# V of a recurrent attention layer: four 32-column tiles of the array at once instead of full-width matmuls with half-empty rows

## The chip, the cores and the metric

The kernel runs on one core of a Trainium2 chip. The metric is the device time of one execution in microseconds, taken as the median of several runs. The kernel before has 3807.35 us (three runs, 3803.83 to 3814.33).

The engines are named as the profile names them: PE is TensorE (matmuls; PEld are its weight loads), DVE is VectorE, ACT is ScalarE, POOL is GpSimd, and SP is the engine whose queue issues the loads of the weights.

## The reference, cut to what matters

Four blocks follow one another on a sequence of 2048 tokens of width 640: A, B, A, B, each with a residual and a layer norm ahead of it. Both A blocks have the same weights, and so have both B blocks.

```python
# A: attention over segments of 32 tokens, with 8 recurrent memory rows (H = 32 heads of Dh = 192)
for s in range(n_seg):                                   # 64 segments
    h = concat([mem, x[s * 32:(s + 1) * 32]])            # 40 rows
    q, k, v = h @ Wq, h @ Wk, h @ Wv                     # each 640 -> 32 x 192
    p = softmax(mask(q @ k.T * scale))                   # 40 x 40 for each head
    o = (p @ v) @ Wo                                     # 32 x 192 -> 640
    mem = o[:8]; out[s] = o[8:]
# B: sliding attention (8 keys, every second one back), 32 heads of 20
q, k, v = split(x @ wqkv); x + attention(q, k, v) @ wo
```

The memory makes the segments of A a chain: segment s + 1 can't begin before segment s has its first 8 output rows. The weights of A (Wq, Wk, Wv, Wo, each 640 x 6144) don't fit on the chip beside the rest, so most of them are loaded again for every segment.

## The kernel before, in words

**Steps and lanes.** One step (`run`, L515 to L554) does segment s of the first A block (lane 0) and segment s - 2 of the second A block (lane 1) together, so that each weight that is loaded serves both lanes: 80 columns, 2 x 40 rows. There are 66 steps, and one more that only ends B. B of both lanes runs within the same step.

**Halves.** The weights of A are cut into 64 "halves" of 480 KB (128 x 1920 bf16): 32 for q and k, 16 for v, 16 for o. 26 of them stay on chip (RESIDENT, L81, spread evenly over the order of use); 38 are loaded in every step through a ring of seven buffers (`half`, L217 to L231). In the first step they come from the inputs and are written to a DRAM copy in the layout of the tiles (`Wr`, L228); afterwards they come from there (L230, on SP's queue). A load can start when the matmuls that read the old contents of its buffer are done.

**The order of a step** is written out by hand in `stages()` (L51 to L63), and TensorE's program follows it exactly. The other engines' instructions are put in order by a scheduler, which keeps to their dependencies. The pieces:

- `q` (16 times, L295): two halves, one of k and one of q, each 15 matmuls of 80 columns (L303); ScalarE evicts the result (L305).
- `s` (4 times, L307): the scores of four units for both lanes (L315, L321), in two other tile forms of the array. VectorE adds the mask (L325), takes the maximum (L327) and subtracts it (L328); ScalarE does the exp (L329); VectorE sums, inverts and scales into Pm (L331 to L333).
- `t` (4 times, L336): TensorE transposes Pm (L340); VectorE copies the upper 64 partitions, those of lane 0, into PT (L342), ScalarE the lower 64, those of lane 1 (L343). The other half of each column of PT stays zero.
- `v` (16 times, L345): one half of Wv. The stationary operand is the 128 columns of ST: two lanes of 64 slots each, of which 40 hold rows and 24 are empty. The moving operand is the weight, 384 columns wide, five matmuls over the contraction (L351). ScalarE evicts the even ones (L355), VectorE the odd ones (L357).
- `pv` (4 times, L360): P times V for four of the v results, in 64-column tiles (L368); ScalarE evicts to ot (L371).
- `o` (16 times, L374): the output projection, one half each (L385), summed in one PSUM tile, acc, over the whole step.
- `e`, `qkv`, `logits`, `wo`, `ln1`, `ln2`: the parts of B. The logits at L444 are computed in four 32-column tiles of the array, each with its own moving operand. Each of the five `e` makes a matmul (L470), a product and a sum on VectorE (L473, L475). GpSimd and VectorE each make one of the two products at L435.

At the end of a step VectorE writes acc's memory rows into the next step's ST (L395). `ln2` (`beta_x`, L495) writes lane 1's new rows there: it takes x2 from `wo` (L486), squares it on GpSimd (L273), sums on VectorE (L275), and needs a matmul, ScalarE's ln and exp and VectorE again (L278 to L292).

**Buffers that the prediction speaks of.** psA, three PSUM buffers, serves q, v and acc (acc holds one from the first `o` to the end of the step). psB, two, serves the parts of B and `t`. vp, six, holds the evicted v.

Of the kernel before, what the change touches and what calls it, by code (L numbers as in the profile page):

```python
# [10 lines left out]
BF16 = mybir.dt.bfloat16  # L11
F32 = mybir.dt.float32
ACT = mybir.ActivationFunctionType
ALU = mybir.AluOpType
# [5 lines left out]
P = 128  # L20
D = 640
NCH = 5
# [3 lines left out]
NM = 8  # L26
SEG = 32
LT = NM + SEG
SLOT = 64
NP_ = 16  # L30
UW = 384
HALF = NCH * UW
NQK = 5
# [12 lines left out]
N_HALVES = 64  # L46
N_RESIDENT = 26
# [2 lines left out]

def stages():  # L51

    plan = [("q", 0), ("q", 1), ("alpha", 0), ("q", 2), ("q", 3), ("ln1", 0)]
    plan += [("q", 4), ("s", 0), ("v", 0), ("q", 5), ("v", 1), ("qkv", 0), ("q", 6), ("t", 0), ("v", 2), ("q", 7), ("v", 3)]
    for g in (2, 3):
        i, j = 4 * g, 2 * (g - 2)
        extra = [[], [], [("logits", 0)], [("input", 0)], []] if g == 2 else [[("e", c)] for c in range(5)]
        plan += [("q", i), ("s", g - 1), ("pv", g - 2)] + extra[0] + [("v", i - 4)] + extra[1] + [("q", i + 1)] + extra[2]
        plan += [("o", 2 * j), ("o", 2 * j + 1)] + extra[3] + [("v", i - 3), ("q", i + 2), ("t", g - 1), ("v", i - 2)] + extra[4]
        plan += [("o", 2 * j + 2), ("o", 2 * j + 3), ("q", i + 3), ("v", i - 1)]  # L60
    plan += [("s", 3), ("pv", 2), ("v", 12), ("v", 13), ("wo", 0), ("o", 8), ("o", 9), ("v", 14), ("v", 15), ("t", 3)]
    plan += [("o", 10), ("ln2", 0), ("pv", 3), ("o", 11), ("store", 0)]
    return plan + [("o", k) for k in range(12, 16)]  # L63


PLAN = stages()


def consumption_order():

    order = []
    for what, i in PLAN:
        if what == "q":
            order += [2 * i, 2 * i + 1]
        elif what in "vo":
            order.append((32 if what == "v" else 48) + i)
    return order


ORDER = consumption_order()  # L80
RESIDENT = {ORDER[(2 * i + 1) * N_HALVES // (2 * N_RESIDENT)] for i in range(N_RESIDENT)}  # L81


def window(ap, l):
# [23 lines left out]
class Kernel:  # L108
    def __init__(self, ctx, tc, A_x, A_mem0, A_Wq, A_Wk, A_Wv, A_Wo, B_wqkv, B_wo, out):
        self.tc, self.nc = tc, tc.nc  # L110
        self.x = A_x[0, :, :]
        self.out = out[0, :, :]
        self.S = A_x.shape[1]
        self.n_seg = self.S // SEG
        self.Wq, self.Wk, self.Wv = (w.rearrange("d h e -> d (h e)") for w in (A_Wq, A_Wk, A_Wv))
        self.Wo = A_Wo.rearrange("h e d -> (h e) d")
        self.B_wqkv, self.B_wo, self.mem0 = B_wqkv, B_wo, A_mem0[0, :, :]
        pool = lambda name, bufs, **k: ctx.enter_context(tc.tile_pool(name=name, bufs=bufs, **k))
        self.cp = pool("consts", 1)
        self.res = pool("res", 1)  # L120
        self.ring = pool("ring", RING)
        self.dram = pool("dram", 1, space=DRAM)
        self.w1 = pool("w1", 1)
        self.w2 = pool("w2", 2)
        self.w3 = pool("w3", 3)
        self.vp = pool("vp", 6)
        self.psA = pool("psA", 3, space=PSUM)
        self.psS = pool("psS", 3, space=PSUM)
        self.psB = pool("psB", 2, space=PSUM)


    def constants(self):
# [12 lines left out]
        for u in range(2):  # L145
            r = slice(SLOT * u, SLOT * (u + 1))
            nc.gpsimd.affine_select(out=m1[r, :], in_=m1[r, :], compare_op=ALU.is_ge, fill=NEG, base=0,
                                    pattern=[[-1, LT]], channel_multiplier=1)
            nc.gpsimd.memset(m1[SLOT * u:SLOT * u + NM, :], 0.0)
        self.maskA = cp.tile([P, LT], BF16, name="maskA")  # L150
        nc.vector.tensor_copy(out=self.maskA[:, :], in_=m1[:, :])

# [23 lines left out]
        self.wqkv = cp.tile([P, NCH, 3 * D], BF16, name="wqkv")  # L176
        self.wo = cp.tile([P, NCH, D], BF16, name="wo")

        self.ST = [cp.tile([P, NCH, 2, SLOT], BF16, name=f"ST{i}") for i in range(2)]
        for t in self.ST:  # L180
            nc.gpsimd.memset(t[:], 0.0)
        self.QK = [cp.tile([P, 12 * LT + SLOT - LT], BF16, name=f"QK{i}") for i in range(NQK)]
        for t in self.QK:
            nc.gpsimd.memset(t[:, 12 * LT:], 0.0)
        self.Pm = [cp.tile([P, 4, 2, SLOT], BF16, name=f"Pm{i}") for i in range(2)]
        for t in self.Pm:
            nc.gpsimd.memset(t[:], 0.0)
        self.PT = [cp.tile([P, 4, 2, 2, LT], BF16, name=f"PT{i}") for i in range(2)]
        for t in self.PT:
            nc.gpsimd.memset(t[:], 0.0)  # L190
        self.zero = cp.tile([P, NCH, SEG], BF16, name="zero")
        nc.gpsimd.memset(self.zero[:], 0.0)
        self.m0T = cp.tile([P, NCH, NM], BF16, name="m0T")
# [101 lines left out]
    def qk(self, i):  # L295
        nc = self.nc
        st = self.ST[self.step % 2]
        ps = self.psA.tile([P, 6, 2, LT], F32, name="qk_ps", tag="A")
        for k in range(2):
            w = self.half(2 * i + k)[:, :].rearrange("p (c n) -> p c n", c=NCH)  # L300
            for m in range(3):
                for c in range(NCH):
                    nc.tensor.matmul(ps[:, 3 * k + m, :, :], lhsT=w[:, c, m * P:(m + 1) * P], rhs=st[:, c, :, 0:LT],  # L303
                                     start=(c == 0), stop=(c == NCH - 1))
        nc.scalar.copy(out=self.QK[i % NQK][:, 0:12 * LT], in_=ps[:, :, :, :].rearrange("p m l t -> p (m l t)"))  # L305

    def scores(self, g):  # L307
        nc = self.nc
# [8 lines left out]
        for j in range(4):  # L317
            q = self.QK[(4 * g + j) % NQK]
            for l in range(2):
                for h in range(2):  # L320
# [9 lines left out]
        sm = self.w2.tile([P, 8], F32, name="sm")  # L330
        nc.vector.tensor_reduce(out=sm[:, :], in_=sb[:, :, :], op=ALU.add, axis=AX.X)  # L331
        nc.vector.reciprocal(out=sm[:, :], in_=sm[:, :])
        nc.vector.tensor_tensor(out=self.Pm[g % 2][:, :, :, 0:LT].rearrange("p a l t -> p (a l) t"), in0=sb[:, :, :],  # L333
                                in1=sm[:, :].unsqueeze(2).to_broadcast([P, 8, LT]), op=ALU.mult)

    def p_transpose(self, g):  # L336
        nc = self.nc
        ps = self.psB.tile([P, 4, 2, SLOT], BF16, name="pt_ps", tag="B")
        for j in range(4):
            nc.tensor.transpose(out=ps[:, j, :, :].rearrange("p h q -> p (h q)"),  # L340
                                in_=self.Pm[g % 2][:, j, :, :].rearrange("p l t -> p (l t)"), identity=self.ident[:, :])
        nc.vector.tensor_copy(out=self.PT[g % 2][0:64, :, :, 0, :], in_=ps[0:64, :, :, 0:LT])  # L342
        nc.scalar.copy(out=self.PT[g % 2][64:128, :, :, 1, :], in_=ps[64:128, :, :, 0:LT])  # L343

    def v(self, i):  # L345
        nc = self.nc
        w = self.half(32 + i)[:, :].rearrange("p (c n) -> p c n", c=NCH)
        st = self.ST[self.step % 2]
        ps = self.psA.tile([P, UW], F32, name="v_ps", tag="A")
        for c in range(NCH):  # L350
            nc.tensor.matmul(ps[:, :], lhsT=st[:, c, :, :].rearrange("p l t -> p (l t)"), rhs=w[:, c, :],  # L351
                             start=(c == 0), stop=(c == NCH - 1))
        vt = self.vp.tile([P, UW], BF16, name="vt")
        if i % 2 == 0:
            nc.scalar.copy(out=vt[:, :], in_=ps[:, :])  # L355
        else:
            nc.vector.tensor_copy(out=vt[:, :], in_=ps[:, :])  # L357
        self.vts[i] = vt

    def pv(self, g):  # L360
        nc = self.nc
        for k in (2 * g, 2 * g + 1):
            ps = self.psS.tile([P, 2, 3, 2, LT], F32, name="o_ps", tag="S")
            for jj in range(2):
                i = 2 * k + jj
                vt = self.vts.pop(i)
                for (n, slot, h, col) in ((0, 0, 0, 0), (0, 1, 0, 64), (1, 0, 0, 128), (1, 1, 1, 192), (2, 0, 1, 256), (2, 1, 1, 320)):
                    nc.tensor.matmul(ps[64 * slot:64 * (slot + 1), jj, n, :, :], lhsT=vt[:, col:col + 64], rhs=self.PT[g % 2][:, i % 4, h, :, :],  # L368
                                     start=True, stop=True, tile_position=(0, 64 * slot))
            ot = self.w3.tile([P, 6, 2, LT], BF16, name="ot")  # L370
            nc.scalar.copy(out=ot[:, :, :, :], in_=ps[:, :, :, :, :].rearrange("p j n l t -> p (j n) l t"))  # L371
            self.ots[k] = ot
# [142 lines left out]
    def run(self):  # L515
# [6 lines left out]
        with tc.manual_schedule(engines={PE}):  # L522
# [7 lines left out]
            for s in range(n_steps + 1):  # L530
# [10 lines left out]
                for what, i in PLAN:  # L541
                    if what in attend and a:
                        attend[what](i)
                    elif what in local and b:
                        local[what]()
                    elif what == "e" and b:
                        self.b_expand(i)
                    elif what == "alpha" and a and s + 1 < self.n_seg:
                        self.alpha_x(s + 1)
                    elif what == "input" and s % 4 == 2 and 4 * (s // 4 + 1) < self.n_seg:  # L550
                        self.input_tile(s // 4 + 1)
# [57 lines left out]
```

## Time and profile before

| what | value |
|---|---|
| median of the runs | 3807.35 us |
| the profiled execution's own time | 3796.64 us |
| its span, from the first to the last instruction | 3794.9 us |
| instructions | 172,681 |
| granted TensorE clock, mean | 0.981 |
| from HBM | 1251.42 MB, 335 GB/s over the span |
| loads `wt<-Wr` of 480 KB, from issue to landing | 2470, median 5.8 us |
| end of a step (L395), first and last of 65 | 149.5 us and 3766.0 us |

The page of the profile gives, in its first part, the busy time of each engine with its share of the span and its number of instructions. Its third part has a line for each DMA queue: packets, megabytes, and the time of its packets as a share of 16 engines' span. Its fourth part follows the chain that ended last backwards from the last instruction, and gives the shares by engine; "issue" there is time in which the engine waited for nothing that the profile shows. A line of a group has its source line, engine, operation, what it writes and reads with shapes, its count, then busy time in us and mean ns of one, then the idle time of the engine just before its instructions, with what ended most of it. A line of the waits reads: who waited, for whom, us in total, times, longest. A line in order of time reads: start in us, length in us, engine, line, operation, count, and in brackets the idle time before it. A line of the chain in order of time reads: start, length, engine, what, line, count.

The mean of one matmul holds its latency, since matmuls are pipelined; the rate is read from the starts of successive ones.

### The profile page before, as it was taken

What the parts mean: (1) busy time and instruction counts of PE and PEld (TensorE: products, weight loads), DVE (VectorE), ACT (ScalarE), POOL (GpSimd) and SP (SyncE); (2) the same over time, 40 slices, a digit from 0 to 9 for tenths busy, and PEclk for the clock granted to TensorE, in tenths of its full rate; (3) what the DMA queues carried; (4) which work ended last, traced back from release to release, by engine and by line L of the source; (5) the groups of instructions that cost most, each with busy time, mean ns of one, the idle gap of its engine ahead of it and who ended that gap; (6) DMA issues with size and microseconds to landing.
All of it is one profiled execution on the core that took longest, in us unless ns stands there. A gap on an engine that the chain in (4) does not pass through costs nothing.

```text
span 3794.9 us, 172681 instructions
## 1 busy us (share of the span) xinstructions
PE 3450.5 (91%) x79035; PEld 2983.5 (79%) x79035; DVE 2024.0 (53%) x4660; ACT 1496.2 (39%) x3213; POOL 372.2 (10%) x475
## 2 busy tenths in 40 slices
PE   5799999999999999999999999999999999999997
PEld 3578887887878888788778887888888888788886
DVE  1255555545545555554555555555555555545555
ACT  1233443444434344343444344444444444444443
POOL 3110010010001001001000100100110010011000
PEclk7899999999999999999999999999999999999998
DMA  9999999999999999999999999999999999999995
GB/s 353 376 329 335 348 341 343 334 338 342 334 335 341 338 349 341 327 350 327 343 336 335 344 338 342 342 339 347 333 348 343 349 338 341 343 332 351 340 352 216
DMA packets 403275, 1283.93 MB, mean 338 GB/s; under 512 B 41704, under 2 KB 83312, under 8 KB 402544
## 3 DMA queue, kind: packets, MB, share of 16 engines
q1 hardware_dynamic: 397200, 1251.58, 91.8%
q0 software_dynamic: 3040, 18.68, 1.2%
q8 instruction: 617, 10.11, 1.1%
q10 hardware_dynamic: 2304, 2.62, 0.2%
q14 instruction: 114, 0.93, 0.1%
HBM read 1251.42 MB, written 21.30 MB: 335 GB/s over the span
## 4 chain that ended last, share of the span: by engine, by line
PE 74%; DVE 16%; DMA 5%; issue 4%; ACT 1%; SPq 1%; POOLq 0%; POOL 0%; ACTq 0%
PE qk_ps L303 26%; PE v_ps L351 20%; PE acc L385 12%; DVE oT L475 5%; DVE prodv L473 4%; PE qkv_ps L428 4%; PE o_ps L368 3%; PE s_ps L321 3%; PE s_ps L315 3%; DMA x_sb<-in_A_x_dram 2%; DVE vt L357 2%; PE y_ps L482 1%; DMA wt<-in_A_Wq_dram 1%; ACT PT L343 1%; DVE sb L325 1%
## 5 line engine op out<-in xcount | busy, mean ns | idle before, releaser
L305 ACT CAST QK<-qk_ps 128x480 bf16<-128x480 f32 x1056 | 588.3, 557 | 1254.0 <-PE qk_ps L303 1243.2
L303 PE MATMUL qk_ps<-ST,wt 128*128 128x80 bf16 x18810 | 866.7, 203 | 102.6 <-issue 28.1
L303 PEld LDWEIGHTS <-wt 128*128 128x128 bf16 x18810 | 770.0, 101 | 149.8 <-issue 96.2
L351 PEld LDWEIGHTS <-ST 128*128 128x128 bf16 x5280 | 469.0, 99 | 341.3 <-issue 100.1
L303 PE MATMUL qk_ps<-ST,res 128*128 128x80 bf16 x12870 | 616.0, 203 | 35.8 <-issue 19.3
L303 PEld LDWEIGHTS <-res 128*128 128x128 bf16 x12870 | 544.8, 101 | 77.9 <-issue 28.6
L351 PE MATMUL v_ps<-wt,ST 128*128 128x384 bf16 x2640 | 525.0, 330 | 75.2 <-DVE vt L357 67.8
L357 DVE CAST vt<-v_ps 128x384 bf16<-128x384 f32 x528 | 289.3, 548 | 541.7 <-PE v_ps L351 541.3
L351 PE MATMUL v_ps<-res,ST 128*128 128x384 bf16 x2640 | 526.0, 330 | 13.4 <-DMA res<-in_A_Wv_dram 7.1
L385 PE MATMUL acc<-ot,wt 128*128 128x80 bf16 x10890 | 494.5, 203 | 14.4 <-issue 8.9
L385 PEld LDWEIGHTS <-wt 128*128 128x128 bf16 x10890 | 437.1, 100 | 29.0 <-issue 9.5
L355 ACT CAST vt<-v_ps 128x384 bf16<-128x384 f32 x528 | 250.6, 475 | 278.5 <-PE v_ps L351 273.4
L371 ACT CAST ot<-o_ps 128x480 bf16<-128x480 f32 x528 | 275.4, 560 | 167.6 <-PE o_ps L368 167.6
L475 DVE TENSOR_REDUCE oT<-prodv 128x64 bf16<-128x512 bf16 x330 | 336.1, 1019 | 2.2
L435 POOL TENSOR_TENSOR prod<-qT,kh 128x1280 bf16<-128x1280 bf16 x66 | 204.4, 3097 | 733.8 <-ACT kh L430 733.8
L325 DVE TENSOR_TENSOR sb<-s_ps,maskA 128x320 f32<-128x320 f32 x264 | 129.3, 490 | 219.4 <-PE s_ps L321 219.4
L385 PE MATMUL acc<-ot,res 128*128 128x80 bf16 x4950 | 234.0, 202 | 7.4 <-DMA res<-in_A_Wo_dram 7.0
L273 POOL TENSOR_TENSOR sq<-x 128x160 f32<-128x160 bf16 x64 | 29.0, 453 | 2106.7 <-DVE x L486 2106.7
L473 DVE TENSOR_TENSOR prodv<-bc_ps,vh 128x512 bf16<-128x512 f32 x330 | 223.0, 676 | 17.3 <-PE bc_ps L470 11.4
L385 PEld LDWEIGHTS <-res 128*128 128x128 bf16 x4950 | 198.1, 100 | 15.2 <-DMA res<-in_A_Wo_dram 7.7
L343 ACT COPY PT<-pt_ps 64x320 bf16<-64x320 bf16 x264 | 111.2, 421 | 197.0 <-DVE PT L342 194.0
L331 DVE TENSOR_REDUCE sm<-sb 128x8 f32<-128x320 f32 x264 | 127.7, 484 | 108.2 <-ACT sb L329 108.2
(112 smaller groups left out, 3343.0 us busy)
## 6 DMA issues: line engine op xcount, KB each, us to landing
wt<-Wr SPq DMA_DIRECT2D x2470, 480.0 KB, 5.8
Wr<-wt POOLq DMA_DIRECT2D x38, 480.0 KB, 6.8
wt<-in_A_Wo_dram SPq DMA_DIRECT2D x11, 480.0 KB, 11.1
wt<-in_A_Wq_dram SPq DMA_DIRECT2D x10, 480.0 KB, 10.8
wt<-in_A_Wk_dram SPq DMA_DIRECT2D x9, 480.0 KB, 11.1
wt<-in_A_Wv_dram SPq DMA_DIRECT2D x8, 480.0 KB, 11.2
res<-in_A_Wv_dram SPq DMA_DIRECT2D x8, 480.0 KB, 11.3
res<-in_A_Wk_dram SPq DMA_DIRECT2D x7, 480.0 KB, 11.3
```

The costliest lines, as they stand in the source:

```text
L303: nc.tensor.matmul(ps[:, 3 * k + m, :, :], lhsT=w[:, c, m * P:(m + 1) * P], rhs=st[:, c, :, 0:LT], start=(c == 0), stop=(c == NCH - 1))
L305: nc.scalar.copy(out=self.QK[i % NQK][:, 0:12 * LT], in_=ps[:, :, :, :].rearrange("p m l t -> p (m l t)"))
L325: nc.vector.tensor_tensor(out=sb[:, :, :], in0=sv, in1=self.maskA[:, :].unsqueeze(1).to_broadcast([P, 8, LT]), op=ALU.add)
L351: nc.tensor.matmul(ps[:, :], lhsT=st[:, c, :, :].rearrange("p l t -> p (l t)"), rhs=w[:, c, :], start=(c == 0), stop=(c == NCH - 1))
L355: nc.scalar.copy(out=vt[:, :], in_=ps[:, :])
L357: nc.vector.tensor_copy(out=vt[:, :], in_=ps[:, :])
L371: nc.scalar.copy(out=ot[:, :, :, :], in_=ps[:, :, :, :, :].rearrange("p j n l t -> p (j n) l t"))
L385: nc.tensor.matmul(self.acc[:, dc, :, :], lhsT=w[:, m % 3, dc * P:(dc + 1) * P], rhs=ot[:, m, :, :], start=(j == 0 and m == 0 and dc == 0) ...
L428: nc.tensor.matmul(ps[:, d, :, :], lhsT=self.wqkv[:, c, kind * D + d * P:kind * D + (d + 1) * P], rhs=self.xnB[:, c, :].rearrange("p (l t) ...
L435: eng.tensor_tensor(out=self.prod[:, :, l, :, :], in0=qT[:, :, l, :].unsqueeze(2).to_broadcast([P, NCH, BW, SEG]), in1=window(kh, l), op=A ...
L473: nc.vector.tensor_tensor(out=pv[:, :, :, :], in0=ps[:, :, :, :], in1=window1(self.vh, c), op=ALU.mult)
L475: nc.vector.tensor_reduce(out=self.oT[:, c, :].rearrange("p (l t) -> p l t", l=2), in_=pv[:, :, :, :].rearrange("p l w t -> p l t w"), op= ...
```

## The change

V is computed with the stationary rows packed tightly. The 80 real rows of both lanes are put into three operands of 32 columns (new tile SV, filled by GpSimd at the start of a step): lane 0's 32 rows, lane 1's 32 rows, and the 16 memory rows of both with 16 empty ones. Each is a 32-column tile of the array, and a fourth tile works at the same time on one of the three operands with another half of Wv. So one round handles a half in full (tiles 0 to 2) and a third of a fourth half (tile 3); three rounds handle four halves. There are 12 rounds a step with 20 matmuls each, where there were 16 with 5 each.

The four halves that serve as the fourth piece are always resident; 22 of the other 60 are, spread evenly, so 38 are still loaded in each step. ScalarE evicts every round. GpSimd copies the rows of the fourth tile (partitions 96 to 127) to their place in the tile vu, of which there is one buffer; vp goes from six buffers to four. The rows of V now stand as lane 0, lane 1, memory, in 96 partitions. Pm's columns follow that order (its last pass on VectorE is split in two), and PT is made by scaling all 96 rows with a column of ones and zeros (own), one for each lane. In the order of a step, the three rounds of a group stand together, behind `pv`, and `wo` moves behind `o` 8.

```diff
+    plan = [("q", 0), ("rows", 0), ("q", 1), ("alpha", 0), ("q", 2), ("q", 3), ("ln1", 0)]
+    plan += [("q", 4), ("s", 0), ("q", 5), ("qkv", 0), ("q", 6), ("t", 0), ("v", 0), ("v", 1), ("v", 2), ("q", 7)]
     for g in (2, 3):
+        i, j, r = 4 * g, 2 * (g - 2), 3 * (g - 1)
+        extra = [[], [("logits", 0)], [], [("input", 0)], []] if g == 2 else [[("e", c)] for c in range(5)]
+        plan += [("q", i), ("s", g - 1), ("pv", g - 2)] + extra[0] + [("v", r), ("v", r + 1), ("v", r + 2)] + extra[1] + [("q", i + 1)] + extra[2]
+        plan += [("o", 2 * j), ("o", 2 * j + 1)] + extra[3] + [("q", i + 2), ("t", g - 1)] + extra[4] + [("o", 2 * j + 2), ("o", 2 * j + 3), ("q", i + 3)]
-    plan += [("s", 3), ("pv", 2), ("v", 12), ("v", 13), ("wo", 0), ("o", 8), ("o", 9), ("v", 14), ("v", 15), ("t", 3)]
+    plan += [("s", 3), ("pv", 2), ("v", 9), ("v", 10), ("v", 11), ("o", 8), ("wo", 0), ("o", 9), ("t", 3)]
     plan += [("o", 10), ("ln2", 0), ("pv", 3), ("o", 11), ("store", 0)]
...
+SHARED = [35, 39, 43, 47]
+ORDER = [h for what, i in PLAN for h in halves(what, i) if h not in SHARED]
+RESIDENT = set(SHARED) | {ORDER[(2 * i + 1) * len(ORDER) // (2 * (N_RESIDENT - 4))] for i in range(N_RESIDENT - 4)}
...
-        self.vp = pool("vp", 6)
+        self.vp = pool("vp", 4)
+        self.vq = pool("vq", 1)
...
-        nc.vector.tensor_tensor(out=self.Pm[g % 2][:, :, :, 0:LT].rearrange("p a l t -> p (a l) t"), in0=sb[:, :, :],
-                                in1=sm[:, :].unsqueeze(2).to_broadcast([P, 8, LT]), op=ALU.mult)
+        for at, n, first in ((0, SEG, NM), (2 * SEG, NM, 0)):
+            nc.vector.tensor_tensor(out=self.Pm[g % 2][:, :, at:at + 2 * n].rearrange("p a (l t) -> p a l t", l=2), in0=sb4[:, :, :, first:first + n],
+                                    in1=sm4.to_broadcast([P, 4, 2, n]), op=ALU.mult)
...
-        nc.vector.tensor_copy(out=self.PT[g % 2][0:64, :, :, 0, :], in_=ps[0:64, :, :, 0:LT])
-        nc.scalar.copy(out=self.PT[g % 2][64:128, :, :, 1, :], in_=ps[64:128, :, :, 0:LT])
+        nc.vector.tensor_scalar(out=pt[0:VT, :, :, 0, :], in0=ps[0:VT, :, :, 0:LT], scalar1=self.own[0:VT, 0:1], scalar2=None, op0=ALU.mult)
+        nc.scalar.activation(out=pt[0:VT, :, :, 1, :], in_=ps[0:VT, :, :, 0:LT], func=ACT.Copy, scale=self.own[0:VT, 1:2])
+
+    def value_rows(self):
+        st = self.ST[self.step % 2]
+        self.nc.gpsimd.tensor_copy(out=self.SV[:, :, 0:2, :], in_=st[:, :, :, NM:LT])
+        self.nc.gpsimd.tensor_copy(out=self.SV[:, :, 2, 0:2 * NM].rearrange("p c (l t) -> p c l t", l=2), in_=st[:, :, :, 0:NM])
...
+    def v(self, r):
+        nc = self.nc
+        g, k = r // 3, r % 3
+        if k == 0:
+            self.shared = self.half(32 + 4 * g + 3)
+            self.vts[4 * g + 3] = self.vq.tile([VT, UW], BF16, name="vu")
+        w = self.half(32 + 4 * g + k)
+        pieces = [(t, t, w) for t in range(3)] + [(3, k, self.shared)]
         ps = self.psA.tile([P, UW], F32, name="v_ps", tag="A")
         for c in range(NCH):
-            nc.tensor.matmul(ps[:, :], lhsT=st[:, c, :, :].rearrange("p l t -> p (l t)"), rhs=w[:, c, :],
-                             start=(c == 0), stop=(c == NCH - 1))
+            for q, t, w in pieces:
+                nc.tensor.matmul(ps[32 * q:32 * (q + 1), :], lhsT=self.SV[:, c, t, :], rhs=w[:, c * UW:(c + 1) * UW],
+                                 start=(c == 0), stop=(c == NCH - 1), tile_position=(0, 32 * q))
         vt = self.vp.tile([P, UW], BF16, name="vt")
-        if i % 2 == 0:
-            nc.scalar.copy(out=vt[:, :], in_=ps[:, :])
-        else:
-            nc.vector.tensor_copy(out=vt[:, :], in_=ps[:, :])
-        self.vts[i] = vt
+        nc.scalar.copy(out=vt[:, :], in_=ps[:, :])
+        nc.gpsimd.tensor_copy(out=self.vts[4 * g + 3][32 * k:32 * (k + 1), :], in_=vt[VT:P, :])
+        self.vts[4 * g + k] = vt
```

`pv` reads vt and PT with 96 rows (VT) for 128, and is otherwise the same. ST loses its empty slots (40 of 64 are kept).

## Prediction

> **What bounds the kernel now.** I read the page first (busy shares, the chain that ended last), then the waits, then one step in order of time.
>
> ```profile
> PE 3450.5 (91%) x79035; PEld 2983.5 (79%) x79035; DVE 2024.0 (53%) x4660; ACT 1496.2 (39%) x3213; POOL 372.2 (10%) x475
> q8 instruction: 617, 10.11, 1.1%
> PE 74%; DVE 16%; DMA 5%; issue 4%; ACT 1%; SPq 1%; POOLq 0%; POOL 0%; ACTq 0%
> L351 PE MATMUL v_ps<-wt,ST 128*128 128x384 bf16 x2640 | 525.0, 330 | 75.2 <-DVE vt L357 67.8
> ```
>
> TensorE carries the time: 91% busy, 74% of the chain. V is 80 matmuls a step (2640 + 2640 over 66 steps). The steps are alike: the eviction at L395 is seen 65 times from 149.5 to 3766.0 us, with 65 steps between, so 55.6 us a step. The first step takes 149.5 us while all weights come from the inputs and 38 tiles are written back; I count no change there.
>
> The two lines to remember are q8 and "issue". PE and PEld have 158,070 instructions; over 617 packets that is 256 to a packet of 16 KB: queue 8 brings TensorE its program, 256 instructions at a time, beside the weights on the same 16 engines. "issue" is TensorE waiting for nothing that the profile shows. The waits and the order of time show where:
>
> ```profile
> PE v_ps L351 <- DVE vt L357: 68.7, 62, 1.5
> PEld L303 <- issue: 124.7, 172, 4.7
> PEld L351 <- issue: 100.1, 138, 1.6
> ```
>
> ```profile
> 1059.56 0.49 PE L303 MATMUL qk_ps<-ST,wt 128*128 128x80 bf16 x9
> 1060.65 0.39 PE L303 MATMUL qk_ps<-ST,wt 128*128 128x80 bf16 x6 [0.60 <-issue]
> ```
>
> The second fence is one weight tile into one PSUM tile, 9 matmuls, a pause of 0.60 us, then the other 6. No data, buffer or engine can be late between them. I counted such pauses in the trace's records of packets and instructions. 182 of the 617 fetches are followed by one, 161 us together (the chain's 4%), and 164 of the 182 fall at the same place modulo 256 instructions. So they are fetches that come late. From the moment a fetch can start (TensorE has entered the block before) to the moment the program goes on, the records give 5.0 us on average, 3.4 to 6.4 for 9 in 10: a queue wait of 2.6 us (median), 1.0 us of transfer (1.1% of 16 engines over 617), 1.4 us more. A block of 256 takes 5.7 us without pauses. Where the fetch takes longer than the block, TensorE pauses, 0.27 us a fetch on average: taking one time from the other, block by block, gives 0.26. By length: 116 blocks under 5.0 us have 0.82 us of pause each, the 152 from 5.0 to 5.5 us 0.25, the 301 above 0.06.
>
> **The change, part by part** (us a step, then times 65).
>
> V matmuls: 80 become 240 in 60 groups of four tiles. One 384-column matmul takes 163 ns start to start (0.81 us for five below). That four column tiles with four different moving operands run at once is shown by L444, the same form with 128 columns:
>
> ```profile
> 1005.41 0.81 PE v_ps L351 x5
> 1012.34 0.39 PE lg_ps L444 x20
> ```
>
> Its records start at 0, 3, 7, 10 ns, then 66, 122, 178, 234: a group of four each 56 ns, as long as one full-array matmul of 128 columns at L470 (56 ns). So a group costs 163 ns and a round 5 x 163 + 10 = 0.825 us. 16 x 0.815 - 12 x 0.825 = **3.15 saved**.
>
> Changes of tile form: the first matmul after one comes 96 ns late (q to scores 132 against 36 ns, pv to V 134 against 33). The order has two more around the first V group, two more around the third, one more behind the fourth, and one less in the second, where the logits follow V in the same form: 4 x 0.096 = **0.4 added**.
>
> Evacuations: VectorE loses 8 x 0.548 us (L357). The wait of V for it goes: 68.7 / 65 = **1.05 saved**. VectorE gains the split of L333: 0.487 us for 320 elements against 0.291 for 128 at L462 leaves some 0.16 fixed, paid once more four times a step, beside matmuls. The two copies of PT keep 320 elements a partition (0.31 and 0.42 us) and get a scale operand, which no row prices; I take nothing, at most 0.1 each. ScalarE gains 4 x 0.475 (L355), at 39% busy.
>
> What is late next: in the changed order ScalarE has ot, ot, exp, then the three vt of a group. The exp waits for three passes of VectorE at 0.49 (L325 to L328). In the shown step, third group, exp ran 1023.72 to 1024.19, so the first vt would end at 1024.7. With acc holding one of three buffers, the third V round needs that buffer at about 1024.0: 0.7 lost. The fourth group has the same, some 0.5. The expansion e4 needs a buffer that L473 frees late (0.4). And wo is now followed by only o, t, o (1.3 us) before ln2, while x2, yT, sq and ssq took 1.4 us (1038.12 to 1039.51) and the copy of PT stands behind ssq on VectorE: some 0.8 before the last pv, against 0.2 now. Together up to 2.4; a pause that falls ahead of such a wait takes its place, so I take **1.0 added**, ends 0 and 2.4.
>
> GpSimd: 12 copies of 32x384. The copies of 160 and 140 elements take 318 and 300 ns, so about 0.52 each; by L273 (720 ns for 320, two inputs) at most 0.9. vu is read a whole group later, in the last group 3 us later, so it is hidden; behind the 3.1 us of L435 the first group's still end before pv. SV's two copies (0.7) delay sq by some 0.3, which ln1 needs four projections later. SP: 38 loads a step as before, 18.68 MB; at 55 us that is 340 GB/s, and the 10 us from 1050 had 391. Weights are no bound.
>
> Program fetches: the order has 178,802 TensorE instructions for 157,682, 10.58 blocks a step for 9.33. Time without pauses: 55.6 - 9.33 x 0.27 = 53.1, then - 3.15 + 0.4 - 1.05 + 1.0 = 50.3, so 4.75 us a block for 5.7. V was where the program rested: 256 instructions of it took 128 x 163 ns = 21 us, now 5.2. A fetch of the measured lengths exceeds a fixed 4.75 us by 0.51 on average; with today's spread of blocks 0.61; I take 0.55 (ends 0.26, as now, and 0.82, as today's short blocks). 10.58 x 0.55 - 2.5 = **3.3 added**.
>
> Sum: -3.15 + 0.4 - 1.05 + 1.0 + 3.3 = +0.5 a step, 33 us. It is made against the profiled execution (3796.64, span 3794.9); the median of the runs is 10.7 above it, and I set the difference on the median: **3840 us**, 0.9% slower.
>
> [...]
>
> **The rivals.**
>
> 1. *The fetches stay as well hidden as now.* Then only their number grows, 82 x 0.26 = 21 us. The rest is -2.8 x 65 = -182. Time 3646. For it: the queue wait is 2.6 of the 5.0 us and hangs on how many weight transfers stand ahead; in the last 16 us of a step the records have 4.3 us, in its first 12 us 5.9. If the new order spreads the weights better, fetches get faster; 0.7 us less in each would be enough. Against it: the bytes a step are the same, and a faster step makes the queue fuller. [...]
>
> 2. *Every block pays as today's short ones do.* 4.75 + 0.82 = 5.57, times 10.58 is 58.9 us, +3.3 a step: 4022. It decides once fetches take 5.4 us throughout, as they do on average in the 116 short blocks, where q and o follow with little V between. For it: the new order has more such stretches. Against it: a pause lets the weight queue run empty.
>
> 3. *The four tiles run one after another*: 240 x 163 ns = 39.1 for 13.0, +26 a step, 5500 us. L444 excludes it but for the width.
>
> **The numbers.** My forecast has 0.52. Its own range comes from 0.2 us either way in the fetch: 59% of the fetches exceed 4.75 us, so 0.2 x 0.59 x 10.58 = 1.25 a step, 3760 to 3920. Rival 1 has 0.23, rival 2 0.23, rival 3 0.02. The range, 3670 to 3980, takes in part of both rivals. A difference of 0.3%, 11 us, is about what can be told from none. Faster: rival 1 and a sixth of the forecast, 0.31; within it 0.10; slower 0.59.
>
> **What would show it.** V at L370 of the changed code: groups of four 163 ns apart (right) or further. The chain's "issue": from 4% to about 10%, 380 us over 699 packets on q8; if it stays under 6%, rival 1 holds. Waits of V for DVE vt gone; waits of the third round for ACT vt, of pv for PT. "PE v_ps" in the chain from 20% to about 15%. I am wrong if issue stays where it is, or if V waits on ScalarE or GpSimd by several us a step.

## The result, and the profile after

The changed kernel has 3965.84 us (median of four runs, 3958.64 to 3972.89) against 3805.59 for the kernel before on the same chip: ratio 1.0436, 95% interval 1.0413 to 1.0459. It is 4.4% slower, where 0.9% slower was forecast; the time lies inside the range, near its upper end. The profiled execution has 3972.89 us, its span 3971.2.

The page of the changed kernel, the same three lines as before: engines, the queue that brings TensorE its program, the chain by engine.

```profile
PE 3389.4 (85%) x89595; PEld 2940.5 (74%) x89595; DVE 1978.7 (50%) x4402; ACT 1628.3 (41%) x3477; POOL 822.5 (21%) x1398
q8 instruction: 700, 11.47, 1.1%
PE 65%; DVE 13%; issue 10%; DMA 7%; ACT 4%; POOL 1%; SPq 1%; POOLq 0%; ACTq 0%
```

TensorE has less to do (3389 us busy for 3451) and the kernel takes longer, so its idle time grew. "issue" has gone from 4% of the chain to 10%, on 700 fetches for 617. That much the prediction named. Not named was that the rest of the chain would not shrink in return: the DVE share fell by 3 points only, ACT rose from 1% to 4% and DMA from 5% to 7%.

The waits of the changed kernel (who waited, for whom, us in total, times, longest):

```profile
PEld L370 <- issue: 196.2, 342, 4.1
PEld L308 <- issue: 148.6, 221, 7.6
PE v_ps L370 <- issue: 84.7, 69, 2.9
PE qk_ps L308 <- issue: 76.5, 83, 2.5
...
PE v_ps L370 <- ACT vt L373: 28.2, 77, 0.5
PE bc_ps L487 <- DVE prodv L490: 26.6, 47, 1.8
PE o_ps L385 <- ACT PT L352: 25.1, 59, 0.5
PE s_ps L320 <- ACT QK L310: 25.1, 64, 0.4
PE pt_ps L348 <- DVE Pm L341: 21.8, 17, 1.4
```

The first four lines are waits for nothing that the profile shows, before V and before q. The 62 waits of V for VectorE (68.7 us) are gone, and so are 16 waits of q for ScalarE's eviction (26 us); the last five lines, 127 us, stand in their place (of pv's for PT 14 us was there before). Three of them stand close together in TensorE's order of time, in the last 12.6 us of a step of the changed kernel:

```profile
2000.95 0.24 PE L320 MATMUL s_ps<-QK 64*64 64x40 bf16 x4 [0.41 <-ACT QK L310]
...
2002.10 0.33 PE L370 MATMUL v_ps<-wt,SV 128*32 128x384 bf16 x3
2002.11 0.33 PE L370 MATMUL v_ps<-res,SV 128*32 128x384 bf16 x1
2002.26 0.33 PE L370 MATMUL v_ps<-wt,SV 128*32 128x384 bf16 x3
...
2002.42 0.33 PE L370 MATMUL v_ps<-wt,SV 128*32 128x384 bf16 x3
...
2004.05 0.34 PE L370 MATMUL v_ps<-wt,SV 128*32 128x384 bf16 x3 [0.32 <-ACT vt L373]
...
2005.53 0.66 PE L499 MATMUL y_ps<-oT,wo 128*128 128x64 bf16 x17
2007.16 0.39 PE L499 MATMUL y_ps<-oT,wo 128*128 128x64 bf16 x8 [0.97 <-issue]
...
2009.88 0.51 PE L385 MATMUL o_ps<-PT,vt 96*64 96x80 bf16 x18 [0.43 <-ACT PT L352]
```

Three tiles of a group start together (and the fourth 10 ns behind), and the groups follow each other at 160 ns (163 by the median of the whole trace): the packed V runs as fast as was said. Then come what the new order brought: the last scores wait 0.41 us for the eviction of the q just before them, because a V round no longer stands between; the third round waits for the first one's eviction; pv waits for PT. And between 17 and 8 matmuls of one line into one tile stands a pause of 0.97 us: a fetch.

For the comparisons below I took three numbers from each trace. **Step**: the time from the first end of a step's memory rows to the last, over the 65 steps between. **Pauses**: breaks of more than 280 ns in TensorE that a fetch ends (they end some 1.4 us after its landing); their sum over 66 gives pauses a step. **Rest**: the step without them.

| kernel | median us | ratio (95%) | step | pauses us (late of all fetches) | rest |
|---|---|---|---|---|---|
| before | 3805.59 | 1 | 55.64 | 161 (182 of 617) | 53.2 |
| changed | 3965.84 | 1.0436 (1.0413 to 1.0459) | 58.48 | 413 (367 of 700) | 52.2 |

So a step grew by 2.84: pauses by 3.8, and the rest fell by only 1.0.

### The profile page after: what moved, and what is told of

It reads as the page before. It is cut to its first block, busy times and chain, and to the rows that moved or that the text cites. A ratio compares the mean times of both kernels' runs of the same rounds, so it can differ in the third digit from the quotient of the medians.

```text
span 3971.2 us, 195526 instructions
## 1 busy us (share of the span) xinstructions
PE 3389.4 (85%) x89595; PEld 2940.5 (74%) x89595; DVE 1978.7 (50%) x4402; ACT 1628.3 (41%) x3477; POOL 822.5 (21%) x1398
## 4 chain that ended last, share of the span: by engine, by line
PE 65%; DVE 13%; issue 10%; DMA 7%; ACT 4%; POOL 1%; SPq 1%; POOLq 0%; ACTq 0%
PE qk_ps L308 25%; PE v_ps L370 14%; PE acc L402 11%; PE qkv_ps L445 3%; DVE oT L492 3%; DVE prodv L490 3%; PE o_ps L385 2%; PE s_ps L326 2%; DMA wt<-Wr 2%; DMA x_sb<-in_A_x_dram 2%; PE s_ps L320 2%; PE bc_ps L487 2%; DVE Pm L341 1%; ACT QK L310 1%; PE y_ps L499 1%
## 5 line engine op out<-in xcount | busy, mean ns | idle before, releaser
L370 PE MATMUL v_ps<-res,SV 128*32 128x384 bf16 x7920 | 760.4, 338 | 60.0 <-issue 58.3
L374 POOL COPY vu<-vt 32x384 bf16<-32x384 bf16 x792 | 408.8, 516 | 1584.3 <-ACT vt L373 1569.7
L370 PEld LDWEIGHTS <-SV 128*32 128x32 bf16 x15840 | 419.7, 99 | 389.8 <-issue 196.2
L308 PE MATMUL qk_ps<-ST,res 128*128 128x80 bf16 x11880 | 573.6, 204 | 31.5 <-issue 22.4
L370 PE MATMUL v_ps<-wt,SV 128*32 128x384 bf16 x7920 | 546.5, 339 | 62.1 <-ACT vt L373 28.2
L373 ACT CAST vt<-v_ps 128x384 bf16<-128x384 f32 x792 | 363.8, 476 | 289.0 <-PE v_ps L370 266.7
L341 DVE TENSOR_TENSOR Pm<-sb,sm 128x256 bf16<-128x256 f32 (+1 forms) x528 | 293.0, 594 | 9.3
L402 PE MATMUL acc<-ot,res 128*128 128x80 bf16 x5940 | 283.2, 203 | 9.6 <-issue 7.3
L352 ACT ACTIVATE PT<-pt_ps,own 96x320 bf16<-96x320 bf16 x264 | 138.1, 523 | 289.0 <-DVE PT L351 281.8
L445 PE MATMUL qkv_ps<-xnB,wqkv 128*128 128x64 bf16 x4950 | 173.9, 197 | 61.4 <-issue 54.0
```

The source lines that it names most:

```text
L341: nc.vector.tensor_tensor(out=self.Pm[g % 2][:, :, at:at + 2 * n].rearrange("p a (l t) -> p a l t", l=2), in0=sb4[:, :, :, first:first + n ...
L370: nc.tensor.matmul(ps[32 * q:32 * (q + 1), :], lhsT=self.SV[:, c, t, :], rhs=w[:, c * UW:(c + 1) * UW], start=(c == 0), stop=(c == NCH - 1 ...
L374: nc.gpsimd.tensor_copy(out=self.vts[4 * g + 3][32 * k:32 * (k + 1), :], in_=vt[VT:P, :])
L402: nc.tensor.matmul(self.acc[:, dc, :, :], lhsT=w[:, m % 3, dc * P:(dc + 1) * P], rhs=ot[:, m, :, :], start=(j == 0 and m == 0 and dc == 0) ...
L445: nc.tensor.matmul(ps[:, d, :, :], lhsT=self.wqkv[:, c, kind * D + d * P:kind * D + (d + 1) * P], rhs=self.xnB[:, c, :].rearrange("p (l t) ...
```

## Experiments

Each ratio is to the kernel before on the same chip. Two theories stood at the start. *Fetches*: the packed V cuts the time that a block of 256 instructions takes, the fetches come late, and that is all of the loss. *Order and waits*: with the V rounds standing together, TensorE meets evictions and softmax passes that it had found done before. e1, e3, e4 and e5 leave part of the computation out (V's fourth piece, or weight columns that are not loaded) and serve for times only. Line numbers in the views below are those of each run's own kernel: in e3 and e4 they are 8 higher than in the kernel that was edited, in e8 one lower.

| kernel | median us | ratio (95%) | step | pauses us (late of all) | rest |
|---|---|---|---|---|---|
| e1 changed, full-width V | 3779.21 | 0.9946 (0.9929 to 0.9963) | 55.46 | 224 (212 of 607) | 52.1 |
| e2 before, more instructions | 3968.12 | 1.0441 (1.0412 to 1.0470) | 58.13 | 335 (313 of 700) | 53.05 |
| e3 changed, small loads | 3664.46 | 0.9643 (0.9619 to 0.9668) | 53.72 | 44 (60 of 700) | 53.05 |
| e4 before, small loads | 3629.00 | 0.9548 (0.9528 to 0.9567) | 53.07 | 23 (34 of 617) | 52.7 |
| e5 e1 with rounds spread | 3684.57 | 0.9691 (0.9666 to 0.9716) | 54.04 | 241 (244 of 607) | 50.4 |
| e6 before, loads in two | 3710.28 | 0.9757 (0.9736 to 0.9778) | 54.18 | 37 (64 of 617) | 53.6 |
| e7 changed, loads in two | 3797.04 | 0.9985 (0.9968 to 1.0003) | 55.56 | 165 (237 of 700) | 53.1 |
| e8 before, the new order | 3959.85 | 1.0417 (1.0394 to 1.0440) | 58.13 | 213 (193 of 617) | 54.9 |
| e9 changed, spread, loads in two | 3722.06 | 0.9793 (0.9767 to 0.9819) | 54.62 | 194 (267 of 700) | 51.7 |
| e10 before, loads in four | 5493.75 | 1.4454 (1.4409 to 1.4498) | 81.71 | 460 | |
| e11 changed, rounds spread | 3913.25 | 1.0291 (1.0256 to 1.0326) | 57.68 | 384 (354 of 700) | 51.9 |

**e1: one full-width matmul for the four tiles.** All else of the change stays: order, evictions, copies. The fourth operand is empty, so the fourth piece of V is left out.

```diff
-            for q, t, w in pieces:
-                nc.tensor.matmul(ps[32 * q:32 * (q + 1), :], lhsT=self.SV[:, c, t, :], rhs=w[:, c * UW:(c + 1) * UW],
-                                 start=(c == 0), stop=(c == NCH - 1), tile_position=(0, 32 * q))
+            nc.tensor.matmul(ps[:, :], lhsT=self.SV[:, c, :, :].rearrange("p t n -> p (t n)"), rhs=w[:, c * UW:(c + 1) * UW],
+                             start=(c == 0), stop=(c == NCH - 1))
```

> The changed kernel with each group of four 32-column matmuls of V replaced by one full-width matmul on the same three operands (the fourth operand is zero): 60 matmuls of V a step for 240, and everything else stays, ScalarE's and GpSimd's evacuations, the buffers and the order of a step. The fourth piece of V is left out (its rows come out as zero), so the result is not the reference's. Theory (TensorE's program fetches come late): 2349 instructions a step, 9.2 blocks of 256 for 10.6; the time without pauses goes from 52.0 to about 51 us a step, a block from 4.9 to 5.55, and the pause a block from 0.60 to about 0.23 us; pauses of some 140 us in all instead of 413, a step of 53 us, 3620 us, 5% under the kernel before. Rival (V waits for ScalarE and GpSimd, and the new order of the step): only the changes of tile form go, some 0.5 us a step, so about 3930 us.

3779 us. Against the changed kernel that is 187 us less, its pauses are 189 us less (224 for 413), and the rest is the same, 52.1 for 52.2. A group of four tiles takes the time of one matmul (163 ns), so little but the number of instructions (and the tile form) differs: **180 TensorE matmuls more a step cost 187 us, and the pauses measure as much**. But the kernel before should have been beaten by far more than 0.5%: it runs 20 more V matmuls a step (3.3 us) and waits for VectorE. The fetches can't be all of it.

**e2: the kernel before with each V matmul cut into three of 128 columns.**

```diff
-            nc.tensor.matmul(ps[:, :], lhsT=st[:, c, :, :].rearrange("p l t -> p (l t)"), rhs=w[:, c, :],
-                             start=(c == 0), stop=(c == NCH - 1))
+            for n in range(3):
+                nc.tensor.matmul(ps[:, n * P:(n + 1) * P], lhsT=st[:, c, :, :].rearrange("p l t -> p (l t)"), rhs=w[:, c, n * P:(n + 1) * P],
+                                 start=(c == 0 and n == 0), stop=(c == NCH - 1), skip_group_check=True)
```

> The kernel before, with each V matmul of 384 columns cut into three of 128, and nothing else changed: 160 more pairs of weight load and matmul a step, as many as the change adds. Three of 56 ns take 168 ns where one takes 163, so 0.4 us a step by themselves. Theory (program fetches): 10.6 blocks a step for 9.3, a block of 5.05 us without pauses for 5.7, 0.45 to 0.6 us of pause each: 2.3 to 3.5 us a step more, the granted clock a little lower, 3980 to 4060 us. Rival (the waits that the change adds are what costs): 0.4 x 65 = 26 us, 3832 us.

It has the changed kernel's 700 fetches and none of its other edits. The page:

```profile
PE 3504.6 (89%) x89595; PEld 3385.1 (86%) x89595; DVE 2040.2 (52%) x4660; ACT 1496.1 (38%) x3213; POOL 372.0 (9%) x475
q8 instruction: 700, 11.47, 1.2%
PE 76%; DVE 10%; issue 7%; DMA 4%; ACT 1%; SPq 1%; POOLq 0%; POOL 0%; ACTq 0%
```

4.4% slower, 2.5 us a step. Three matmuls of 128 columns take 168 ns (three times 56) for 163, so 80 of them account for 0.4; pauses rose by 2.6, and "issue" from 4% to 7%. (The two make 3.0; in return V's waits for VectorE's vt fell from 68.7 to 27.3 us, as pauses took their place.) So 83 more blocks of 256 instructions brought 174 us more of pauses (335 for 161).

**e3 and e4: both kernels with loads of 7/15 of the bytes.** The matmuls read the loaded columns again, so their number and shape stay (those lines are left out here).

```diff
-            self.nc.sync.dma_start(out=t[:, :], in_=self.Wr[h][:, :])
+            self.nc.sync.dma_start(out=t[:, 0:CUT], in_=self.Wr[h][:, 0:CUT])
...
```

> The changed kernel with weight loads of 896 of 1920 columns after the first step; the matmuls read those columns again and again, in the same number and shape, so the result is not the reference's. Theory: the program's packets no longer stand behind weights, a fetch takes 3.5 us or less for 5.1, pauses nearly vanish (under 80 us in all), and a step takes about 52 us: 3540 us. Rival: the weights are no bound and the time stays within 1% of 3966 us.

> The kernel before with the same smaller loads. Theory: its pauses of 161 us go as well, so a step falls from 55.6 to about 53.2 us, 3650 us, and the changed kernel with small loads is some 3% faster than this one: the saving in V then shows. Rival: no change here, 3805 us, and the two kernels stand to one another as with full loads, 4% apart the other way.

With less traffic the pauses all but go: 44 us of 413 in the changed kernel, though it has the same 700 fetches. After the first 200 us a fetch now takes 3.4 us on average for 5.0, its queue wait 0.9 us for 2.7 (median). So the weights' traffic is what makes a fetch late: with 7/15 of their bytes, 1.8 of the 2.7 us in the queue went. (The packets are shorter here too, 1792 bytes for 3840; e7 below shortens them with all the bytes kept, and has 165 us.) Yet the changed kernel is still the slower of the two, 3664 for 3629. Of these 35 us 21 are pauses that are left; the point is that its rest, forecast 2.8 us lower, isn't lower at all (53.05 for 52.7). The chain of e3 by engine:

```profile
PE 54%; DVE 32%; ACT 6%; DMA 4%; issue 3%; POOL 1%; SPq 1%; POOLq 0%; ACTq 0%
```

TensorE's waits in e3, between 300 and 3500 us:

```profile
PE pt_ps L356 <- DVE Pm L349: 85.3, 60, 1.4
PE v_ps L378 <- ACT vt L381: 44.0, 115, 0.5
PE s_ps L328 <- ACT QK L318: 39.9, 72, 1.7
PE qkv_ps L453 <- ACT qT L455: 29.7, 60, 0.6
PE o_ps L393 <- ACT PT L360: 25.9, 60, 0.4
```

The chain of e4, the kernel before with these loads:

```profile
PE 77%; DVE 17%; DMA 3%; SPq 1%; ACT 1%; issue 1%; POOLq 0%; POOL 0%; ACTq 0%
```

And TensorE's waits in e4, over the same stretch:

```profile
PE v_ps L359 <- DVE vt L365: 90.1, 60, 1.5
PE qk_ps L311 <- DVE ST L403: 20.2, 61, 0.3
PE o_ps L376 <- ACT PT L351: 12.8, 61, 0.2
```

Over the 60 steps of that stretch, TensorE's matmuls wait 4.4 us a step for other engines in e3 and 2.1 in e4. The wait for vt that the change removes (1.5 us here) is paid back more than twice, the largest part of it at pt_ps: the transposes wait 1.4 us for Pm in every step. In the changed kernel itself the same line shows 21.8 us, 17 times: there a pause ahead of it takes its place. *Fetches* alone fell with e1 and e3; *order and waits* had to be measured by itself.

**e8: the kernel before, all of its V rounds as they were, in the change's order** (four V together behind `pv`, `wo` behind `o` 8).

```diff
...
-        plan += [("q", i), ("s", g - 1), ("pv", g - 2)] + extra[0] + [("v", i - 4)] + extra[1] + [("q", i + 1)] + extra[2]
+        plan += [("q", i), ("s", g - 1), ("pv", g - 2)] + extra[0] + [("v", r), ("v", r + 1), ("v", r + 2), ("v", r + 3)] + extra[1] + [("q", i + 1)] + extra[2]
...
-    plan += [("s", 3), ("pv", 2), ("v", 12), ("v", 13), ("wo", 0), ("o", 8), ("o", 9), ("v", 14), ("v", 15), ("t", 3)]
+    plan += [("s", 3), ("pv", 2), ("v", 12), ("v", 13), ("v", 14), ("v", 15), ("o", 8), ("wo", 0), ("o", 9), ("t", 3)]
```

> The kernel before with the order of a step that the change has, V's four matmul groups together where the change has three rounds, and wo behind o 8; V itself, its evictions and its 16 halves as before. Theory (the order): waits of TensorE grow by 1.5 to 2.3 us a step, the pauses shrink a little as blocks get longer; 3860 to 3940 us. Rival (the order costs nothing): 3805 us.

4.2% slower, 157 us, with not one instruction more. The rest grew by 1.7 us a step and the pauses by 0.8, though the number of fetches is the same. V in one piece leaves the stretches of q, o and small pieces between without any of it, so that their blocks are short: after the first 200 us, and without the pause behind a block, e8 has 16 blocks under 4 us, with 1.9 us of pause each, and 149 above 7 us; the kernel before has none and 65. **The order alone, on the kernel before, costs about as much as the instructions alone (157 and 167 us).** Of its waits, three lines are those of the changed kernel; the old wait of V for VectorE's vt (the second line) is halved:

```profile
PE bc_ps L469 <- DVE prodv L472: 44.9, 67, 1.8
...
PE v_ps L350 <- DVE vt L356: 34.4, 54, 0.7
...
PE s_ps L314 <- ACT QK L304: 26.1, 66, 0.7
PE v_ps L350 <- ACT vt L354: 23.4, 69, 0.5
```

**e5 and e11: the rounds spread again.** e5 is e1 (full width) and e11 the changed kernel, both with the three rounds of a group put back between other pieces, about where V had stood before, and `wo` again ahead of `o` 8.

```diff
...
-        plan += [("q", i), ("s", g - 1), ("pv", g - 2)] + extra[0] + [("v", r), ("v", r + 1), ("v", r + 2)] + extra[1] + [("q", i + 1)] + extra[2]
-        plan += [("o", 2 * j), ("o", 2 * j + 1)] + extra[3] + [("q", i + 2), ("t", g - 1)] + extra[4] + [("o", 2 * j + 2), ("o", 2 * j + 3), ("q", i + 3)]
+        plan += [("q", i), ("s", g - 1), ("pv", g - 2)] + extra[0] + [("v", r)] + extra[1] + [("q", i + 1)] + extra[2]
+        plan += [("o", 2 * j), ("o", 2 * j + 1)] + extra[3] + [("q", i + 2), ("t", g - 1), ("v", r + 1)] + extra[4]
+        plan += [("o", 2 * j + 2), ("o", 2 * j + 3), ("q", i + 3), ("v", r + 2)]
...
```

> The kernel of the first experiment (one full-width matmul in place of four tiles; the fourth piece of V left out) with its twelve rounds put back between the other pieces, as the kernel before has them: one behind pv, one behind t, one behind the last q of a group, for three together. Theory (the new order of the step costs, since V no longer stands between q and the scores that need its last eviction, nor between t and what waits for it): the waits of TensorE fall from 4 us a step to about 2.3, and with 9.2 blocks a step the pauses stay at some 2.5 us; 52.8 us a step, 3620 us. Rival (the order is no cause, the evacuations by ScalarE and GpSimd are): 3780 us, as with the rounds together.

> The changed kernel as it is (four tiles, 240 matmuls of V a step), with its twelve rounds put back between the other pieces as in the fifth experiment. Theory (order and program fetches both cost, each by itself): the waits fall by 2 us a step, more changes of tile form cost 1.2, the pauses stay near 0.55 us a block; 3880 to 3920 us, so 200 us or more above the same order with full-width matmuls (3685), of which 30 to 80 are changes of tile form and the rest program fetches. Rival (with V between the other pieces the fetches are hidden again): 3780 us.

In full width the spread order gives 95 us (e1 to e5), the rest from 52.1 to 50.4. With four tiles it gives 53 us, and the rest moves from 52.2 to 51.9 only. There a round that stands alone has up to two changes of tile form, which the trace has at 93 to 96 ns: V stands in 11 places for 4, so up to 7 x 0.19 = 1.3 us a step (an estimate from that row), near the 1.4 that spreading saves less here. So grouping V saves changes of form and exposes waits, and spreading does the reverse. The pauses are 384 us for 413.

**e6, e7, e9, e10: the same bytes in more and smaller loads**, to see whether the fetch's queue is the packet in front of it. A load's packet is 3840 bytes and takes 149 ns; in two it is 1920 and 79 ns, in four 960 and 44 ns (medians). e6, e7 and e9 have the edit below, e10 the same with four parts.

```diff
-            self.nc.sync.dma_start(out=t[:, :], in_=self.Wr[h][:, :])
+            for a in (0, HALF // 2):
+                self.nc.sync.dma_start(out=t[:, a:a + HALF // 2], in_=self.Wr[h][:, a:a + HALF // 2])
```

> The kernel before with each weight load after the first step cut into two of half the columns, so that the packets are 1920 bytes for 3840: the same bytes, twice the packets. Theory (a program fetch waits behind a number of packets that its DMA engine has already taken): the queue wait of a fetch falls from 2.6 to about 1.5 us, the pauses from 161 to under 60 us, 3700 us. Rival (it waits for bytes, or the more frequent issues cost as much): 3800 us or more.

> The changed kernel with the same loads cut in two. Theory: pauses from 413 to some 150 us; part of that comes back as waits for data, 3740 us. Rival: 3966 us or more.

> The changed kernel with its rounds spread and each weight load cut in two: both costs of the change reduced, the whole computation done. Theory: against the changed kernel with loads in two (3797) the waits fall by 2 us a step and tile forms cost 1.2 more, pauses shrink with the spreading; 3720 to 3770 us. If V's saving of 3.15 us a step came through in full, it would be under 3650 us.

> The kernel before with each weight load cut in four (packets of 960 bytes). Theory (the fetch waits behind a number of packets): the queue wait falls again, to about 1.2 us, and the last 37 us of pauses go, 3680 us, unless the packets' own overhead makes the weights late. Rival: the load engines pay a fixed time for a packet, so the weights come too late, waits of TensorE for DMA wt appear, over 3760 us.

e6, the kernel before with this one line cut in two, is 2.4% faster than it and the fastest of those that do the whole computation. Its chain:

```profile
PE 69%; DMA 15%; DVE 12%; ACT 1%; SPq 1%; issue 1%; POOLq 0%; POOL 0%; ACTq 0%
```

"issue" goes from 4% to 1%, pauses from 161 to 37 us, though a fetch still takes 4.39 us on average (5.0 before) and its queue wait only fell from 2.6 to 2.0, less than by half as the packets did. The changed kernel gains more from it (413 to 165 us of pauses in e7) and comes out level with the kernel before. e9 has the rounds spread and the loads in two, and is not faster than e6: its rest is 1.9 us a step lower (51.7 for 53.6), and its pauses are 2.4 higher (194 for 37 us). **The change does save in the rest; the pauses that come with its instructions take it back even with faster fetches.**

e10 shows where cutting ends. Its chain by engine:

```profile
SPq 39%; DMA 31%; PE 24%; issue 5%; DVE 1%; ACT 0%; POOLq 0%; POOL 0%; ACTq 0%
```

SP's queue of e10 in order of time:

```profile
1999.73 12.25 SPq L231 DMA_DIRECT2D wt<-Wr  x22
```

22 issues take 12.25 us here, 0.557 each; over a longer stretch, 2000 to 2060 us, 113 take 60.31, 0.534 each. Four to a load and 38 loads are 152 a step, which makes 81 us of the step's 81.7: SP's issuing is the bound. A fetch's queue wait falls further, to 0.8 us (median), but the DMA engines also have less to do (232 GB/s from HBM for 335). The 460 us of breaks in its row are not shown to be late fetches: in the kernel before 164 of 182 stand at one place modulo 256 instructions, here no place has more than 16 of several hundred.

## Why the prediction was wrong, point by point

- *V, 3.15 saved.* Right: groups stand 163 ns apart.
- *Changes of tile form, 0.4 added.* Right in size: 93 to 96 ns each for the 96 taken.
- *Program fetches, 3.3 added.* Right in mechanism, near in size. 700 fetches for 699, 413 us of pauses for 380, 0.59 us a block for 0.55, "issue" 10% for about 10%; 330 of the 367 pauses stand at one place modulo 256 instructions. A fetch takes 5.0 us, as before. Measured as pauses a step it is 3.8, not 3.3: 0.5 short. e1 prices the instructions by themselves at 187 us. After the first 200 us a block of 4 to 5 us costs 0.82 us, where it cost 0.79 before, and one of 5 to 5.5 us 0.19 for 0.23: the price of a block by its length stayed. What changed is that there are 331 blocks of 4 to 5 us for 123, and 56 under 4 us where there was none.
- ***The step that failed: the wait for vt saved 1.05, the new waits cost 1.0.*** With V and the tile forms as said, the two should have left the rest 2.8 us lower. It fell by 1.0, so in place of −0.05 stands about +1.75. The wait for vt did go. The new ones, priced at 1.0 with an upper end of 2.4, took 2.8 by this difference. 1.8 too little here and 0.5 in the fetches are 2.3 us a step, 150 us: that and the forecast's 33 make 183, and the profiled executions differ by 176. e3 against e4 shows the same with the pauses and the half clock (7 and 0 us between 200 and 3500) nearly out of the way: TensorE's matmuls wait 2.3 us a step more, where −0.05 was forecast.
- *What that term missed.* I went through the changed order looking for what is late at V's new place (the third round, pv, the expansion; all three showed) and not for what V had covered at its old places. In the old order V was the filler between q and the scores and ahead of t; e8, with only the places changed, has 1.7 more in the rest, about the size of the gap (it is the kernel before, so this is a likeness and not a split of the 1.75). The scores' wait for the last q (25.1 us, 64 times) and the transposes' wait for Pm were not in my list.
- *VectorE's split of Pm, 0.16 beside matmuls.* The two parts take 591 and 598 ns for one of 487: 0.70, four times a step. In e11 they take 455 and 273, 0.24 together; so the split's own price was near, and the rest comes with the grouped order. The unsplit Pm also grows there, from 487 to 572 in e8. What slows it was not tried.
- *The clock.* In no term. Between 200 and 3500 us the records have TensorE at half its clock for 34 us before and 123 after; in them successive matmuls of q start 67 ns apart for 36. The 89 more cost up to half of that, 0.8 us in each of the 57 steps there. Without it the new waits come to 2.0, twice what I took and inside its ends. The busy times between 1000 and 3000 us (the last three columns are granted clock, DMA share and GB/s), of the kernel before:

```profile
1000.00:3000.00 2000.00, 1856.34 (x43050) 1612.05 (x43048) 1102.83 (x2542) 813.87 (x1751) 182.83 (x216) 1.00 0.95 340
```

The same view of the changed kernel:

```profile
1000.00:3000.00 2000.00, 1736.76 (x46387) 1510.07 (x46384) 1034.52 (x2279) 841.38 (x1801) 405.43 (x684) 0.98 0.91 324
```

The clock is 0.98 for 1.00, and TensorE and the DMA engines both do less in the same time. Half clock did not go with the amount of pauses alone: e8 has 78 us of it, e1 82 and e11 85, while e2, with 335 us of pauses, has 44 and e9, with 194, has 3. It went with their place, as far as the records tell. In the records the clock changes on a grid of 3.41 us. In the changed kernel TensorE's matmuls stood idle for half or more of 39 of these stretches at full clock, and 26 of the 39 were followed by half clock; of all the others 6 were. In the kernel before it is 6 of 9, in e2 12 of 16, and e9 has one such stretch. So most stretches of half clock here came behind one in which pauses and waits fell close together (26 of 32 in the changed kernel); no run tested this by itself.
- *GpSimd hidden.* Right: 516 ns a copy, for 520; none of the changed kernel's waits of TensorE above is one for GpSimd.
- *The rivals.* 1 (fetches hidden) fell: fetches are as long as before (5.0 us) and pauses grew (161 to 413 us). 2 (every block as today's short ones, 0.82) fell as a mechanism, at 0.59 a block, though its time, 4022, lies nearer to the result than mine. My own range, 3760 to 3920, does not hold the result; the wider one does because it took in part of this rival, so that is luck. 3 fell by the groups' 163 ns.

What stays open: the +1.75 is not split into single waits. From 200 to 3700 us TensorE's matmuls wait 131 us for VectorE and ScalarE in the kernel before and 146 in the changed one; its weight loads wait under 1 us and 60, partly at the same moments. With the clock's 0.8 that is about the right size, but e8 prices the order only as a whole. Waits and pauses hide each other, as e3 showed: with the pauses gone, the rest came out higher (53.05) than with them (52.2).

## What to carry to other kernels

Before splitting a matmul into several, compare the time that 256 TensorE instructions take with the time of a program fetch under the kernel's DMA load (here 5 us): in the changed kernel a block of 4 to 5 us cost 0.82 us of pause and one of 5 to 5.5 us 0.19. Here the fetches hid behind wide matmuls of 163 ns: cut in three (e2), they left 335 us of pauses for 161. When independent work is moved, list what it covered at its old place, not only what is late at the new one; running the old kernel in the new order costs one experiment and prices that alone. And where the program is late beside a queue's large packets, cut those first (two loads for one gave 2.4% here), as long as the issuing queue keeps up (with four for one, at 0.53 us an issue, it did not).

## What the runs showed of the hardware that was not expected

- Loads cut in two, with packets of 1920 bytes for 3840 and the same bytes in total, took the program's pauses from 161 to 37 us; that there are twice as many loads was not tried apart. A packet took 79 ns for 149 and a fetch's queue wait was 2.0 us for 2.6 (medians); what the wait is made of was not shown.
- An issue on SP takes some 0.53 us in e10 (113 in 60.31 us), so that this kernel can't be fed by loads of 120 KB from one queue: it is 45% slower.
- Half-clock stretches of TensorE appear in the middle of a kernel that it keeps 85% busy, 123 us between 200 and 3500 for 34 in the kernel before, and cost up to some 44 us of the 160 (an estimate: half of the 89 more). 26 of 39 stretches of 3.41 us in which its matmuls stood idle for half the time or more were followed by one.
